# Sixteen weight forms spread over GpSimd's pairs, two weight steps moved into the attention, and a new order in the first in-projection

## The chip, the cores and the metric

The kernel runs on one core of one Trainium2 chip. The metric is device microseconds (us) of one execution; a comparison takes the median of several.

## The reference

Two layers, one after the other. The first is attention with routing: 4 batches of 8 heads, 768 positions, 64 features, 16 centroids for each head.

```
q_assign = argmax(einsum(q_n, c_n)); k_assign = argmax(einsum(k_n, c_n))
scores = where(q_assign == k_assign, scale * q @ k.T, -1e9)
attn   = softmax(scores) ;  attn_out = attn @ v
```

The heads' outputs, side by side, are x (3072 tokens by 512 features). The second layer is `h = x @ w_in` (512 by 2048), `g = h * erf(softplus(h))`, `out = g @ w_out` (2048 by 512). w_in and w_out come as float64, the other inputs and the output are float32.

## The kernel before

**Order.** Every instruction is recorded through a helper (`InOrder`, lines 119 to 132) which keeps each engine's instructions in the order of the program, so nearly all rows of the profile have line L127, and one reads them by tile. Tiles wait for one another through pools of few buffers: a tile can be written again when its last reader is done.

**Attention.** Heads are taken two at a time: 16 pairs (p = 0 to 15), each in six periods (i = 0 to 5; function `period`, line 1367, called from the loop at 1538). Each period handles two "units", tiles of 128 keys, against 768 queries; periods 0 to 2 are one half of a pair and 3 to 5 the other. What a period does for units u and u + 1:

- `step_ahead` and `maxima_step` make the softmax's shifts: TensorE writes candidates into the tile `wide`, which has a single buffer, and VectorE reduces them into `nmx`. `into_rows` turns a half's shifts into rows (`least`, `least_rows`) that SP's queue copies into `qm`.
- `products` is the first product q k (TensorE into `sc`, two buffers), and `scores` adds the rows of mask and shift (`sc<-qm,km`).
- `curve` is the exponential (ScalarE, `sc` to `pr`).
- For the two units before (u - 2, u - 1), `accumulate` adds up `pr` on GpSimd into `more_out`, for the denominators, and `attend` is the second product `pr` v (TensorE into `turned`).
- In periods 0 and 3 `divide` ends the half before: a product of the sums with a tile of minus ones (`turned<-more_out,minus`), logarithm and exponential on ScalarE (`inv`), the division on VectorE (`den`, `turned`, `more_out`), and the writes to `x_dram`.

**Weight steps.** w_in and w_out, float64 bit patterns, come as 32 steps of 512 KB, each made into float32 from the high and low words (`w_steps`, line 280): `fetch` (DMA), `size` and `rest` (ScalarE), `bounded` (VectorE), `sign` (ScalarE), `shifted` (VectorE), and `summed` (GpSimd, an integer addition), which then fetches the next step into the place that came free. Two steps are done in each pair. The last `N_LATE` = 4 are done after the attention.

**Forms.** The two matrix products use seven products in the place of eight (and in chunk 0 of the second layer, 26), so operands are first added and subtracted: `left_forms` (line 653) for w_in and `right_forms` (662) for x, four operations of 128 x 512 each. They are taken from a list `forms`: one on VectorE where the table `FORMS` says so (pair 15, periods 0, 3, 4, 5: one, two, two, two), and one on GpSimd where `POOL_FORMS` says so (pairs 8 to 15, period 1, ahead of that period's `accumulate`). The list holds w_in's columns f = 0, 2, 4, then those of x. What is left of it runs after the loop, and the four for f = 6 run on GpSimd behind the last sums of the attention.

**After the attention.** `hidden(0, 0)` and `hidden(0, 1)` make the first half of chunk 0's hidden layer, four `block`s each. A block is seven products into `bank` tiles (six buffers, then the two of `turned`), the evictions that add them up, and after each product one entry of the list `aside_work`: this list sets by its order where the late weight steps, the gate's curve (`split_gate`, `gate_work`) and the forms of w_out (`middle_forms26`, `late_forms26`) stand between the evictions. `idle(n)` is n empty entries. Between blocks 0 and 1 `finish_attention` does the last division and `next_forms26` records forms of w_out on GpSimd. The forms of w_out are chains of fills on SP (`g_more<-w_out`, `x_own<-w_out`), DMAs issued by GpSimd that add onto what was filled (`onto_by_dma`, line 803), and stores (`b_dram<-x_own`, line 794). `project26(0)` (line 1236) is the second matrix product of chunk 0. Its product `bank<-g_more,g` uses what the chains made.

Of the kernel before, what the change touches and what calls it, by code (L numbers as in the profile page):

```python
# [9 lines left out]
F32 = mybir.dt.float32  # L10
# [9 lines left out]
P = 128  # L20
# [23 lines left out]

UP = 2.0**16
FORMS = {15: {0: 1, 3: 2, 4: 2, 5: 2}}
POOL_FORMS = {p: (1,) for p in range(8, 16)}
BIG = 2.0**60
FLOOR = 2.0**50
EPS = 2.0**-70  # L50
NPT = NJ + 2
N_LATE = 4
PLACE_OF = [n % 5 for n in range(25)] + [2, 3, 2]
LAST_X = 11
MASKS = {(0, 2): ("k", 0), (2, 3): ("q", 0), (2, 2): ("k", 1), (3, 2): ("q", 1)}
FIRST_MASKS = {(2, 0): ("k", 0), (2, 1): ("q", 0), (2, 2): ("k", 1), (5, 3): ("q", 1)}
# [79 lines left out]
def kernel(  # L136
# [141 lines left out]


    w_steps = []  # L280
    for c in range(0, DFF, LC):
        for r in range(DM // P):
            w_steps.append((w_in[:, r, c : c + LC], moe_w_in[r * P : (r + 1) * P, 2 * c : 2 * (c + LC)]))
    for f in range(HF):
# [260 lines left out]
    def scores(u, rows=Q):  # L545

        p, half, j = units[u]
        st = pairs[p]
        sc = sc_of[u]
        assert ("shift", half) in st  # L550
        for e in range(2):
            r = slice(e * D, (e + 1) * D)
            r = slice(r.start, r.start + rows)
            te.matmul(
                sc[:, e, 0:HW], lhsT=st["km"][r, j * P : (j + 1) * P],
                rhs=st["qm"][r, half * HW : (half + 1) * HW], start=False, stop=True,
            )
# [95 lines left out]
    def left_forms(engine, a11, a12, a21, a22, new):  # L653

        return [
            functools.partial(plus_of, new[0], a21, a22, engine),
            functools.partial(minus_of, new[1], new[0], a11, engine),
            functools.partial(minus_of, a21, a11, a21, engine),
            functools.partial(minus_of, new[2], a12, new[1], engine),
        ]  # L660

    def right_forms(engine, b11, b12, b21, b22, new):

        return [
            functools.partial(minus_of, new[0], b12, b11, engine),
            functools.partial(minus_of, new[1], b22, new[0], engine),
            functools.partial(minus_of, b12, b22, b12, engine),
            functools.partial(minus_of, new[2], new[1], b21, engine),
        ]
# [10 lines left out]
    def w_in_parts(f, n):  # L680
        c1, c2 = slice(f * P, (f + n) * P), slice((HF + f) * P, (HF + f + n) * P)
        return (
            w_in[:, 0:HK, c1], w_in[:, HK:, c1], w_in[:, 0:HK, c2], w_in[:, HK:, c2],
            [more_in[:, i, :, c1] for i in range(3)],
        )

    def x_parts(n):
        x = x_of[n]
        return (
            x[:, 0:HK, 0:HT], x[:, 0:HK, HT:], x[:, HK:, 0:HT], x[:, HK:, HT:],  # L690
            [x_more[:, i] for i in range(3)],
        )
# [65 lines left out]
    def idle(n):  # L758
        return [lambda: None] * n
# [598 lines left out]
            run(steps)  # L1358
        return steps

    forms = []
    for f in range(0, HF - 2, 2):
        forms += zip(*(left_forms(e, *w_in_parts(f, 2)) for e in (ve, ge)))
    routing = [iter(())]
    part = [iter(())]
# [1 line left out]
    def period(p, i):  # L1367
        u = 2 * NJ * p + 2 * i
        n1, n2 = 2 * p - 1, 2 * p
        early = lambda n: 0 <= n < N_EARLY  # L1370

        def mask(place):
            which = (MASKS if p else FIRST_MASKS).get((i, place))
            if which:
                return masks(p + 1, *which, turned[0 if i in (0, 5) else 1], place == 2)
            return lambda: None

        if u > 0:
            for which in turns if i in (0, 3) else ():
                turn(*which)  # L1380
                turns.remove(which)
            if i == 3 and p:
                similarities(p + 2)
                routing[0] = choose(p + 2, turned[0], True)
            step_ahead(p, 2 * i)
            if i == 3 and p:
                next(routing[0], None)
            if i == 2:
                transposes(p + 2, "k")
        mask(0)()  # L1390
        if i == 0 and early(n1 - 1):
            sign(n1 - 1)
        elif i == 3 and early(n1):
            sign(n1)
        if i == 4:
            next(routing[0], None)
        next(part[0], None)
        if i == 0 and p:
            run(routing[0])
            transposes(p + 2, "q")  # L1400
        if u == 2:
            next(routing[0])
        products(u)
        mask(3)()
        products(u + 1)
        mask(1)()
        second = step_ahead(p, 2 * i + 1, True) if u > 0 else iter(())
        next(second, None)
        rows = D if u == 0 or u + NJ + 2 >= len(units) else Q
        scores(u, rows)  # L1410
        next(second, None)
        next(second, None)
        next(part[0], None)
        if i == 5:
            next(routing[0], None)
        scores(u + 1, rows)
        later = mask(2)
        if i == 3 and not p:
            similarities(p + 2)
            routing[0] = choose(p + 2, turned[0], True)  # L1420
        if i == 0:
            later()
            curve(u)
        else:
            curve(u)
            later()
        curve(u + 1)
        if u == 0:
            step_ahead(0, 1)
            similarities(1)  # L1430
            routing[0] = choose(1, turned[0])
            next(routing[0])
            next(routing[0])
            vectors(1, "q")
            vectors(1, "k")
        if i == 0 and early(n1 - 1):
            bounded(n1 - 1)
            shifted(n1 - 1)
        elif i == 1 and early(n1):
            size_and_rest(n1)  # L1440
        elif i == 5 and early(n2):
            rest(n2)
        for _ in range(min(len(forms), FORMS.get(p, {}).get(i, 0))):
            forms.pop(0)[0]()
        if i == 3:
            if not p:
                next(routing[0], None)
            if early(n1):
                bounded(n1)
                shifted(n1)  # L1450
        elif i == 1:
            load(p + 1, "v", v, vp)
            if p == 0:
                run(routing[0])
                transposes(2, "q")
        elif i == 4:
            vectors(p + 2, "k")
            vectors(p + 2, "q")
        if u > 0:
            if i == 1 and early(n1 - 1):  # L1460
                summed(n1 - 1)
            elif i == 4 and early(n1):
                summed(n1)
            if i in POOL_FORMS.get(p, ()) and forms:
                forms.pop(0)[1]()
            for w in (u - 2, u - 1):
                accumulate(w)
            for w in (u - 2, u - 1):
                attend(w)
            if i == 3:  # L1470
                next(routing[0], None)
            if i % HJ == 0:
                part[0] = divide(u - 1)
                next(part[0])
        if i == 3 and early(n2):
            size(n2)
# [61 lines left out]
    for p in range(NPAIR):  # L1538
        for i in range(HJ * 2):
            period(p, i)  # L1540
        if p == LAST_X:
            load_x(0)
        if p == LAST_X + 2:
            forms += zip(*(right_forms(e, *x_parts(0)) for e in (ve, ge)))
    for work, _ in forms:
        work()
    u = len(units)
    for w in (u - 2, u - 1):
        accumulate(w)
    for w in (u - 2, u - 1):  # L1550
        attend(w)
    last = divide(u - 1)
    for work in left_forms(ge, *w_in_parts(HF - 2, 2)):
        work()
    attention.close()

    psb = pool("psb", 6, space=PSUM)
# [7 lines left out]
        run(last)  # L1565
        banks[:] = [None] * 6 + turned

    places = [gsp.tile([P, 3, FG, P], F32, name="g_more").rearrange("p a j t -> p (a j t)") for _ in range(2)]
    places += [outp.tile([P, 2, DM], F32, name="osb").rearrange("p h m -> p (h m)") for _ in range(2)]
    place_of.update({N_EARLY + i: places[i][:, 0 : 2 * LC] for i in range(N_LATE)})  # L1570
    for i in range(N_LATE):
        fetch(N_EARLY + i)
# [9 lines left out]
    def all_sums():  # L1582
# [3 lines left out]

    first_half, first_products = split_gate(0, 0)
    second_half, second_products = split_gate(0, 1)
    aside_work += (
        idle(3) + sum((weights(n) for n in range(N_LATE)), []) + [first_half, all_sums, *middle_forms26(), *idle(3), *first_products]  # L1590
    )
    hidden(0, 0, {0: lambda: (finish_attention(), next_forms26())})

    def last_half():
        finish_aside()
        first_steps = [functools.partial(left_step, 0, x) for x, step in enumerate(LEFT_STEPS) if step[0] < 0]
        aside_work.extend(gate_work(0, 1, 0, first_steps, 6))

    aside_work += [second_half, *late_forms26(), *idle(4), *second_products]
    hidden(0, 1, {1: last_half}, first=ve.tensor_copy)  # L1600
    finish_aside()
    project26(0)
    last_of_x = x_more[:, 2, 0, 0:1]
# [42 lines left out]
```

## Time and profile before

| | |
|---|---|
| median of 3 runs | 950.81 us (950.78 to 950.81) |
| profiled execution | 950.88 us |
| its span, first to last instruction | 949.2 us |
| granted TensorE clock, mean | 1.000 |
| DMA traffic | 123.17 MB, mean 130 GB/s |
| GpSimd's sums for the denominators, x128 | 217.6 us, 1700 ns each |
| VectorE's reductions of `wide`, x189 | 179.1 us, 948 ns each |
| the exponentials, x192 | 148.4 us, 810 ns each |
| second products, x3072 | 145.2 us, 330 ns each |

The page has one row for each engine (busy time, share of the span, instructions), then the span in 40 slices, the DMA queues, the chain of work that ended last, and the groups of instructions. PE is TensorE's matmuls, PEld its weight loads, DVE VectorE, ACT ScalarE, POOL GpSimd, SP SyncE. A row of a timeline has the start in us, the duration in us (of all, where instructions of one kind follow each other and the row says xN), engine, line, operation, output <- inputs and shape, and in brackets the idle time of the engine before it and who ended it. Starts and durations of neighbours overlap by up to a tenth of a us.

### The profile page before, as it was taken

To read this page: it belongs to the slowest core of one execution; us is meant where nothing else is said; L and a number is where in the kernel's file an instruction comes from. 1 tells how busy PE (TensorE), PEld (TensorE's weight loads), DVE (VectorE), ACT (ScalarE), POOL (GpSimd) and SP (SyncE) were. 2 spreads that over 40 slices of the span, in tenths; PEclk is the share of its full clock that TensorE was granted. 3 is DMA by queue.
4 is the path that set the end of the run, shared out by engine and by line. 5 is a ranking of instruction groups with operands and counts; after the bars stand their busy time and mean duration, and the time that the engine had idled before them with its cause. 6 is when DMAs were issued, how large, how long until landed. Compare 5 with 4: busy or idle time off the path is not lost.

```text
span 949.2 us, 22323 instructions
## 1 busy us (share of the span) xinstructions
PE 940.0 (99%) x8758; PEld 707.4 (75%) x8758; DVE 789.3 (83%) x1418; ACT 545.9 (58%) x808; POOL 504.5 (53%) x357
## 2 busy tenths in 40 slices
PE   8999999999999999999999999999999999999998
PEld 3555555555555555588888888998999899989987
DVE  8888888888888887879886688688868977897887
ACT  3677777777777776475513643654257236525541
POOL 1688888888888888899109211360063016103600
PEclk9999999999999999999999999999999999999999
DMA  9354445444443621132876247353454436343533
GB/s 211 78 114 113 111 112 113 111 113 112 111 112 67 157 58 36 26 119 112 220 235 233 100 117 205 119 182 111 156 158 143 133 116 208 112 154 123 156 111 111
DMA packets 176344, 123.17 MB, mean 130 GB/s; under 512 B 132592, under 2 KB 143344, under 8 KB 176240
## 3 DMA queue, kind: packets, MB, share of 16 engines
q1 hardware_dynamic: 171872, 116.34, 42.9%
q0 software_dynamic: 1872, 4.98, 3.0%
q8 instruction: 69, 1.13, 0.5%
q10 hardware_dynamic: 2496, 0.43, 0.2%
q14 instruction: 35, 0.29, 0.1%
HBM read 91.78 MB, written 23.33 MB: 121 GB/s over the span
## 4 chain that ended last, share of the span: by engine, by line
PE 93%; DVE 2%; ACT 2%; issue 1%; POOL 1%; DMA 1%; SPq 0%; DVEq 0%; POOLq 0%; ACTq 0%
PE bank L127 40%; PE turned L127 31%; PE sc L127 16%; PE wide L127 6%; POOL more_out L127 1%; DVE g L127 1%; DVE nmx L127 1%; ACT a_s L127 0%; DMA g_more<-in_moe_w_out_dram 0%; ACT L127 0%; ACT w_out L127 0%; ACT osb L127 0%; SPq L127 0%; DMA qm<-least_rows 0%; ACT g_more L127 0%
## 5 line engine op out<-in xcount | busy, mean ns | idle before, releaser
L127 POOL TENSOR_TENSOR more_out<-more_out,pr 128x768 f32<-128x768 f32 x128 | 217.6, 1700 | 17.1 <-ACT pr L127 7.5
L127 DVE TENSOR_REDUCE nmx<-wide 128x2 f32<-128x512 f32 (+2 forms) x189 | 179.1, 948 | 46.9 <-PE wide L127 45.9
L127 ACT ACTIVATE pr<-sc 128x768 f32<-128x768 f32 x192 | 148.4, 810 | 82.1 <-PE wide L127 74.4
L127 PE MATMUL turned<-pr,in_v 128*32 128x193 f32 x3072 | 145.2, 330 | 0.0
L127 POOL TENSOR_TENSOR g<-g 128x512 f32<-128x512 f32 x36 | 47.1, 1308 | 180.7 <-DVE g L127 178.9
L127 PEld LDWEIGHTS turned<-pr,in_v 128*32 128x32 f32 x3072 | 90.2, 109 | 51.2 <-issue 26.5
L127 DVE TENSOR_TENSOR g<-g 128x512 f32<-128x512 f32 x132 | 90.8, 688 | 22.3 <-PE bank L127 11.8
L127 PE MATMUL sc<-qT,kT 64*128 64x384 f32 x528 | 98.5, 485 | 0.0
L127 DVE TENSOR_TENSOR g<-bank,g 128x256 f32<-128x256 f32 (+1 forms) x128 | 64.6, 531 | 16.1 <-PE bank L127 9.5
L127 PE MATMUL bank<-g_more,g 128*128 128x256 f32 x320 | 75.7, 379 | 0.0
L127 PE MATMUL bank<-x_own,w_in 128*128 128x128 f32 (+1 forms) x440 | 74.0, 310 | 0.0
L127 ACT ACTIVATE a_s<-g 128x1024 f32<-128x1024 f32 x38 | 39.5, 1053 | 57.8 <-POOL g L127 45.9
L127 POOL TENSOR_TENSOR more_out<-pr,pr 128x768 f32<-128x768 f32 x32 | 59.1, 1847 | 20.4 <-ACT pr L127 20.3
L127 DVE TENSOR_TENSOR g<-a_s,g 128x512 f32<-128x512 f32 x76 | 68.0, 913 | 0.7 <-ACT a_s L127 0.7
L127 PEld LDWEIGHTS bank<-g_more,g 128*128 128x128 f32 x320 | 60.7, 190 | 8.5 <-DVE g L127 0.2
L127 PEld LDWEIGHTS bank<-x_own,w_in 128*128 128x128 f32 x440 | 63.1, 191 | 4.6 <-issue 0.6
L127 PE MATMUL wide<-kv,qv 64*128 64x256 bf16 (+2 forms) x378 | 64.7, 327 | 1.1 <-ACT km L127 0.6
L127 PE MATMUL bank<-w_out,g 128*128 128x256 f32 x280 | 64.5, 379 | 0.0
L127 PEld LDWEIGHTS <-qv 64*128 64x128 bf16 x384 | 23.1, 93 | 53.3 <-issue 38.3
L127 ACT ACT_TABLE_LOAD x40 | 51.3, 1283 | 19.4 <-DVE g L127 18.8
L127 PE MATMUL wide<-km,qm 64*128 64x256 bf16 (+4 forms) x378 | 62.2, 326 | 0.0
L127 PEld LDWEIGHTS sc<-qT,kT 64*128 64x128 f32 x528 | 46.4, 187 | 19.0 <-issue 1.8
(241 smaller groups left out, 1993.4 us busy)
## 6 DMA issues: line engine op xcount, KB each, us to landing
g_more<-b_dram SPq DMA_DIRECT2D x52, 512.0 KB
g_more<-w_dram SPq DMA_DIRECT2D x84, 256.0 KB
x_own<-in_moe_w_in_dram SPq DMA_DIRECT2D x13, 512.0 KB
in_v<-in_v_dram SPq DMA_DIRECT2D x32, 192.0 KB
x_dram<-more_out SPq DMA_DIRECT2D x128, 48.0 KB
x_own<-x_dram SPq DMA_DIRECT2D x6, 1024.0 KB
in_k<-in_k_dram SPq DMA_DIRECT2D x59, 96.0 KB
in_q<-in_q_dram SPq DMA_DIRECT2D x58, 96.0 KB
```

Source lines behind the costliest of these rows:

```text
L127: ins = getattr(self.engine, name)(*args, **kw)
```

## The change

- GpSimd's forms stand in pairs 5 to 13 (before 8 to 15). The list holds the 16 forms of w_in, f = 0, 2, 4, 6. The four of x have a list of their own, `x_forms`, on VectorE, which is emptied first in pair 15.
- What is left of the forms of w_in in the list runs on GpSimd after `next_forms26` (before: four right after the attention's last sums).
- `N_LATE` is 2: steps 28 and 29 (w_out) are done in pairs 14 and 15. In pair 15 both are summed in period 4. The order of w_in's steps takes the columns 0, 1024, 512, 1536. The two late steps both use the tiles `osb`.
- In pair 15, period 3, both `attend`s stand before `scores`.
- In the first in-projection, the `aside_work` has 8 entries of weight steps (before 16), then the sums, the middle forms, the gate's curve and its products, each of which is followed by an empty entry; `last_half` comes after block 0 of `hidden(0, 1)` and no longer empties the list.

In the order of the engines, that leaves TensorE the same instructions, of which only `attend` and `scores` of that one period change places. On VectorE, pair 15 has between its eighth and ninth reduction `bounded` and `shifted` of step 28 and one form of x (before: one form of w_in), and in period 3 two forms of x and `bounded` and `shifted` of step 29 ahead of the division. On GpSimd the sums of steps 28 and 29 stand ahead of the sums of the last two units but two. On SP two fetches of w_out move into pair 14, and in `project26(0)` a store `b_dram<-x_own` moves ahead of a fill `g_more<-w_out`. ScalarE does the size of step 28 in pair 14, period 3, its rest in period 5, its sign in pair 15, period 0, and those of step 29 in periods 1 and 3.

```diff
-POOL_FORMS = {p: (1,) for p in range(8, 16)}
+POOL_FORMS = {p: (1,) for p in range(5, 14)}
-N_LATE = 4
-PLACE_OF = [n % 5 for n in range(25)] + [2, 3, 2]
+N_LATE = 2
+PLACE_OF = [n % 5 for n in range(25)] + [2, 3, 2, 3, 2]
...
-    for c in range(0, DFF, LC):
+    for c in (0, DFF // 2, LC, DFF // 2 + LC):
...
-    forms = []
-    for f in range(0, HF - 2, 2):
+    forms, x_forms = [], []
+    for f in range(0, HF, 2):
...
+        attends_first = p == NPAIR - 1 and i == HJ
+        if attends_first:
+            for w in (u - 2, u - 1):
+                attend(w)
         scores(u, rows)
...
-        for _ in range(min(len(forms), FORMS.get(p, {}).get(i, 0))):
-            forms.pop(0)[0]()
+        for _ in range(FORMS.get(p, {}).get(i, 0)):
+            x_forms.pop(0)() if x_forms else forms.pop(0)[0]()
...
-            if i == 1 and early(n1 - 1):
+            if i == (1 if p < NPAIR - 1 else 4) and early(n1 - 1):
                 summed(n1 - 1)
-            elif i == 4 and early(n1):
+            if i == 4 and early(n1):
                 summed(n1)
...
-            for w in (u - 2, u - 1):
+            for w in () if attends_first else (u - 2, u - 1):
                 attend(w)
...
-            forms += zip(*(right_forms(e, *x_parts(0)) for e in (ve, ge)))
-    for work, _ in forms:
-        work()
+            x_forms += right_forms(ve, *x_parts(0))
...
-    for work in left_forms(ge, *w_in_parts(HF - 2, 2)):
-        work()
...
-    places = [gsp.tile([P, 3, FG, P], F32, name="g_more").rearrange("p a j t -> p (a j t)") for _ in range(2)]
-    places += [outp.tile([P, 2, DM], F32, name="osb").rearrange("p h m -> p (h m)") for _ in range(2)]
+    places = [outp.tile([P, 2, DM], F32, name="osb").rearrange("p h m -> p (h m)") for _ in range(2)]
...
+    def spread(work):
+        return sum(([w, *idle(1)] for w in work), [])
+
     aside_work += (
-        idle(3) + sum((weights(n) for n in range(N_LATE)), []) + [first_half, all_sums, *middle_forms26(), *idle(3), *first_products]
+        idle(3) + sum((weights(n) for n in range(N_LATE)), []) + [all_sums, *middle_forms26(), *idle(1), first_half, *idle(8)]
     )
-    hidden(0, 0, {0: lambda: (finish_attention(), next_forms26())})
+    aside_work += spread(first_products)
+
+    def next_forms():
+        next_forms26()
+        for _, work in forms:
+            work()
+
+    hidden(0, 0, {0: lambda: (finish_attention(), next_forms())})
 
     def last_half():
-        finish_aside()
...
-    aside_work += [second_half, *late_forms26(), *idle(4), *second_products]
-    hidden(0, 1, {1: last_half}, first=ve.tensor_copy)
+    aside_work += [second_half, *late_forms26(), *idle(4), *second_products[:2], *idle(1), *second_products[2:]]
+    hidden(0, 1, {0: last_half}, first=ve.tensor_copy)
```

## The prediction

> **What bounds the kernel now.** First the page, for which engine is full; then windows of stages for idle TensorE; then timelines of each idle stretch.
>
> ```profile
> span 949.2 us, 22323 instructions
> PE 940.0 (99%) x8758; PEld 707.4 (75%) x8758; DVE 789.3 (83%) x1418; ACT 545.9 (58%) x808; POOL 504.5 (53%) x357
> PE 93%; DVE 2%; ACT 2%; issue 1%; POOL 1%; DMA 1%; SPq 0%; DVEq 0%; POOLq 0%; ACTq 0%
> ```
>
> TensorE is busy for 940.0 of 949.2 us, and 93% of the chain that ends last is its own work. The change leaves its 8758 matmuls as they are and only lets four groups of the last pair change places. So the time can move by no more than what TensorE's gaps gain or lose, and the table of windows (columns: window, its length, then busy time and count of PE, PEld, DVE, ACT and POOL; clock, DMA share, GB/s) says where gaps are.
>
> ```profile
> 220.00:240.00 20.00, 20.00 (x290) 10.69 (x289) 17.37 (x30) 16.01 (x24) 16.94 (x12) 1.00 0.43 93
> 361.00:373.00 12.00, 11.72 (x167) 6.20 (x161) 8.89 (x14) 9.03 (x14) 10.81 (x8) 1.00 0.14 32
> 385.00:402.00 17.00, 16.70 (x255) 9.54 (x254) 13.69 (x16) 8.30 (x12) 14.40 (x9) 1.00 0.11 25
> 420.00:440.00 20.00, 19.10 (x88) 16.18 (x87) 16.12 (x30) 12.79 (x14) 20.00 (x16) 1.00 0.20 80
> ```
>
> In a middle pair there is none (20.00 of 20.00). Pair 14 leaves 0.28 us, pair 15 leaves 0.30, the start of the second half 0.90. That is all there is to win near the change, at most about 3 us; what can be lost has no such limit.
>
> **Term 1: pairs 5 to 7 get a form on GpSimd, pair 14 loses its own.** The list of waits for pairs 8 to 13, and the timeline of pair 14:
>
> ```profile
> PEld turned L127 <- POOL more_out L127: 1.2, 6, 0.2
> 370.77 0.16 PEld L127 LDWEIGHTS turned<-more_out,minus 128*32 128x32 f32 x8 [0.66 <-POOL more_out L127]
> 360.60 1.28 POOL L127 TENSOR_TENSOR w_in<-w_in 128x512 f32<-128x512 f32 x1
> 369.02 1.69 POOL L127 TENSOR_TENSOR more_out<-more_out,pr 128x768 f32<-128x768 f32 x1
> ```
>
> The six pairs that have a form each show one wait of 0.2 us for GpSimd's sums of the exponentials, ahead of the product that spreads the denominators. Three more such pairs cost between 0 and 3 x 0.2 = 0.6; the window above that has a form in it has no idle TensorE, so I take +0.1. In pair 14 the same wait is 0.66: GpSimd's last sum ends at 369.02 + 1.69 = 370.71, and TensorE starts at 370.77. Without the 1.28 us form that chain ends earlier, and the wait falls to at most the others' 0.2: −0.46 (between 0 and −0.66). Late next is the row of weight loads itself. Weight step 28's size and rest, new in this pair, are ScalarE's, which is idle for 3 of these 12 us; its fetch stands on SP behind reads of v that are needed a pair later. I cost both at nothing; without that cover a fetch of 512 KB would delay a v tile, and the first row of the next pair would show it.
>
> **Term 2: three operations of VectorE ahead of a maximum in pair 15.** Before, one form stands between the eighth and ninth reductions; after, `bounded` and `shifted` of step 28 and a form of x, and GpSimd has no form there.
>
> ```profile
> 380.92 1.23 DVE L127 TENSOR_REDUCE nmx<-wide 128x2 f32<-128x1024 f32 x1 [1.14 <-PE wide L127]
> 380.92 1.52 ACT L127 ACTIVATE pr<-sc 128x768 f32<-128x768 f32 x2 [2.19 <-PE wide L127]
> 381.66 1.28 POOL L127 TENSOR_TENSOR more_in<-w_in 128x512 f32<-128x512 f32 x1
> 382.06 1.43 DVE L127 TENSOR_TENSOR more_in<-w_in,more_in 128x512 f32<-128x512 f32 x1
> 382.90 2.27 POOL L127 TENSOR_TENSOR more_out<-pr,pr 128x768 f32<-128x768 f32 x1
> 383.41 0.68 DVE L127 TENSOR_REDUCE nmx<-wide 128x2 f32<-128x512 f32 x1
> 384.20 0.38 PE L127 MATMUL wide<-kv,qv 64*128 64x512 bf16 x2
> 358.35 0.88 DVE L127 TENSOR_SCALAR w_out<-w_out 128x512 f32<-128x512 f32 x2
> 370.07 1.39 DVE L127 TENSOR_SCALAR w_out<-w_out 128x512 f32<-128x512 f32 x2
> 396.74 0.69 DVE L127 TENSOR_TENSOR more_in<-w_in,more_in 128x512 f32<-128x512 f32 x1
> 389.81 2.16 DVE L127 TENSOR_TENSOR w_in<-w_in 128x512 f32<-128x512 f32 x1
> 385.90 7.62 POOL L127 TENSOR_TENSOR more_out<-more_out,pr 128x768 f32<-128x768 f32 x4 [0.74 <-ACT pr L127]
> ```
>
> The ninth reduction ends at 383.41 + 0.68 = 384.09 and TensorE's next `wide`, which has one buffer, starts at 384.20: it waits for nothing else. A VectorE form takes 0.69 alone but 1.43 or 2.16 beside GpSimd; two scalar operations take 0.88 alone and 1.39 beside it, ending 0.75 after GpSimd's 370.71. So of the two engines one stands still until the other's instruction is done. In after, the eighth reduction ends at 382.1; `bounded` runs to 382.58 (0.44). The exponentials end at 382.44, and GpSimd's first sum, which before had to follow its own form, is ready then and runs next: about 1.7 us (as at 369.02), to 384.3. Then `shifted` 0.44, the next sum not being ready before 385.9; the form 0.69; the reduction, 0.6 to 0.68 in: 384.3 + 0.44 + 0.69 + 0.68 = 386.1 at worst, with overlapped starts (rows begin up to 0.1 before the last ends) 385.85. Against 384.09 that is **+1.75**. The least is GpSimd after all three: 382.1 + 0.88 + 0.69 + 0.68 = 384.35, +0.25. I take +1.75, since between two waiting engines the row of four sums beside two VectorE forms (1.9 each where 1.69 is the sum alone; 1.73 and 2.16 where 0.69 is) shows them taking turns. Nothing gives it back in the pair: scores, exponentials and GpSimd's sums all follow that `wide`.
>
> In the Trainium skill, "SBUF — State Buffer", section "Who interferes with whom", states that VectorE and GpSimd share a port pair under an exclusive lock for a whole instruction, and that issue order decides who blocks. The rows agree that one blocks entirely; who comes first at 382.5 no run here shows yet. By the skill's rule taken strictly, an instruction of VectorE in the queue before 382.44 would hold GpSimd off, and the sum would have +0.25 here: rival B.
>
> **Term 3: second products ahead of scores at the end of pair 15's first half.**
>
> ```profile
> 391.59 0.50 PE L127 MATMUL sc<-qm,km 64*128 64x384 bf16 x4 [0.26 <-DMA qm<-least_rows]
> 393.57 0.16 PEld L127 LDWEIGHTS turned<-more_out,minus 128*32 128x32 f32 x8 [0.42 <-POOL more_out L127]
> ```
>
> The scores waited 0.26 for the transfer of the shift rows. With the second products (1.51 us) ahead of them that wait is hidden. But the product behind waits for GpSimd: the sums end at 385.90 + 7.62 = 393.52, and it starts at 393.57. Second products and scores both stand before it, in either order, so the gap moves and stays: 0, between −0.4 and +0.2 (the exponentials start later, and ScalarE has slack). The two x forms and step 29 behind it are on a VectorE that idles 3.1 us there; the two integer sums now in this half, on GpSimd, are in term 4.
>
> **Term 4: the first blocks after the attention.** Timelines of 405 to 448:
>
> ```profile
> 396.81 8.41 POOL L127 TENSOR_TENSOR more_out<-more_out,pr 128x768 f32<-128x768 f32 x4 [1.37 <-ACT pr L127]
> 405.26 0.37 ACT L127 COPY g<-bank 128x256 f32<-128x256 f32 x1 [4.63 <-POOL more_out L127]
> 407.15 1.03 PE L127 MATMUL bank<-x_more,w_in 128*128 128x256 f32 x4
> 371.59 1.29 POOL L127 TENSOR_TENSOR w_out<-w_out,x_own 128x512 int32<-128x512 int32 x1 [0.88 <-PE turned L127]
> 426.65 0.35 ACT L127 COPY g<-turned 128x256 f32<-128x256 f32 x1
> 435.09 0.73 PEld L127 LDWEIGHTS turned<-x_more,more_in 128*128 128x128 f32 x4 [0.76 <-DVE g L127]
> 436.76 0.73 PEld L127 LDWEIGHTS turned<-x_own,w_in 128*128 128x128 f32 x4 [0.95 <-DVE g L127]
> 447.19 0.73 PEld L127 LDWEIGHTS bank<-x_own,w_in 128*128 128x128 f32 x4 [0.20 <-DVE g L127]
> ```
>
> The gaps at 435 to 447 are TensorE waiting for VectorE's evictions, which all stand behind ScalarE's copy at 426.65, after the gate's curves. With two weight steps fewer before the curves and the gate's products spread out, that copy comes some 2.3 us earlier (two steps are 4 ScalarE operations of about 1 us, two of them hidden beside GpSimd). 2.3 covers the largest gap, so 0.76 + 0.95 + 0.20 = 1.91 less some 0.1 that remains: −1.82. On the other side, two sums of 1.29 now stand ahead of GpSimd's last sums of pair 15, whose end (396.81 + 8.41 = 405.22) releases the first eviction at 405.26; that end comes some 1.8 later (2.6 less the 0.8 of idle before them), the eviction too, and the seventh product, at 407.15, needs its bank after it: 0.45 lost. Sum **−1.37**, between −1.82 and 0.
>
> **Term 5: the chain of w_out's forms.** Before, the four forms of column 6 ran at once after the attention; now they run behind the forms of w_out, with two sums fewer in their way.
>
> ```profile
> 406.98 1.27 POOL L127 TENSOR_TENSOR more_in<-more_in,w_in 128x512 f32<-128x512 f32 x1
> 450.35 1.87 POOL L127 DMA_DIRECT2D more_out<-x_own  x2
> 466.24 1.09 SPq L810 DMA_DIRECT2D g_more<-w_out  x1
> 467.92 0.72 SPq L794 DMA_DIRECT2D b_dram<-x_own  x1
> 473.66 0.84 POOL L127 DMA_DIRECT2D g_more<-x_own  x1 [9.71 <-PE bank L127]
> g_more<-x_own POOLq DMA_DIRECT2D x1, 512.0 KB, 4.6
> 480.11 1.89 PE L127 MATMUL bank<-g_more,g 128*128 128x256 f32 x8
> ```
>
> Four forms (4 x 1.27 = 5.1) move from a time in which GpSimd would have waited for the division to one in which it works; two sums of 1.29 go: its last issue, at 450.35, comes 0.6 to 1 later. On SP the fill of `g_more` (466.24) now stands behind the store (467.92 + 0.72): up to 2.4 later. The transfer that adds onto it lands at 473.66 + 4.6 = 478.26, and TensorE needs it at 480.11: 1.85 of slack, of which term 4 takes 1.37 by bringing TensorE forward. Left is 0.5; for a delay of 1.3, the middle of 0 to 2.4, the loss is **+0.8**. Ends: 0, and (1.0 + 2.4) − 0.5 = 2.9.
>
> The Trainium skill, "DMA: Bandwidth & Descriptors", section "Queues, rings and completion order", has descriptors of one issuing engine consumed in ring order on each DMA engine. By that the fill would wait out the store's 512 KB, and the loss would lie nearer its upper end; rival D.
>
> **The sum.** +0.1 − 0.46 + 1.75 + 0 − 1.37 + 0.8 = +0.82. The profiled execution took 950.88 (its span and 1.7 around it), 0.07 above the median of 950.81. 950.88 + 0.82 = **951.7**. The other edits (column order of w_in's steps, places, names) add no instruction.
>
> **Rivals.**
> - **B: VectorE's three operations go first.** Term 2 is +0.25, GpSimd's end is as before, term 4 is −1.5: 0.1 − 0.46 + 0.25 − 1.5 + 0.8 = −0.8, so **950.1**. For it: VectorE is already at work when GpSimd becomes ready. Against: the alternation at 385.90.
> - **D: slower by the chain of w_out.** Place: the product at 480.11. It decides once the fill's data come more than 0.5 us late; from there each us is lost one for one. At the upper end 2.9 in the place of 0.8: **953.8**. For it: the store is now ahead in the same queue. Against: 473.66 waited, by its row, for a product, so the fill may have had room.
> - **E: the covers all hold.** Term 2 +0.25, term 3 −0.4, term 4 −1.82, term 5 zero: 0.1 − 0.46 + 0.25 − 0.4 − 1.82 = −2.3, so **948.6**.
> - That the swap of term 3 does nothing, because GpSimd ends last, is in the forecast.
>
> **How the numbers follow.** A difference under 0.2%, 1.9 us, is about what a measurement can't tell from none. Chances: forecast 0.53, B 0.17, D 0.18, E 0.12. Faster by more is most of E, 0.10; slower by more is D, 0.18; 0.72 remain. The range leaves out half of D above and most of E below: 949.0 to 953.6.
>
> **What would show it.** Right: at the `wide` before the second unit of pair 15, TensorE idle for about 1.7 us behind a reduction near 386; no GpSimd wait of 0.66 in pair 14; no gap for VectorE at 435 to 447; a wait of under 1 us for `g_more` near 480. Wrong: the first sum on GpSimd beginning after the x form (B); a gap of 2 us or more at the first products with `g_more` (D); or any gap over 0.5 us in pairs 5 to 7, for which no row here stands.

## The result, and the profile after

The changed kernel takes 952.13 us (median of 22 runs, 951.67 to 952.46), the kernel before 950.78 beside it (22 runs, 950.41 to 951.34): ratio 1.0014, 95% interval 1.0008 to 1.0020. It is 1.35 us slower. The interval leaves out 1, so the loss is clear of the noise, but it is under the 0.2% that the prediction set as its bound. The profiled execution took 952.18, before 950.88.

The page after: the same matmuls, the same busy TensorE, a span 1.3 longer, so all of the difference is idle TensorE.

```profile
span 950.5 us, 22319 instructions
PE 940.0 (99%) x8758; PEld 707.5 (74%) x8758; DVE 790.5 (83%) x1417; ACT 546.3 (57%) x808; POOL 504.7 (53%) x358
PE 96%; DVE 2%; POOL 1%; issue 1%; ACT 0%; DVEq 0%; POOLq 0%
```

The table of windows of the changed kernel, with one more than before (after the length: busy time and count of PE, PEld, DVE, ACT, POOL; clock, DMA share, GB/s):

```profile
361.00:373.00 12.00, 12.00 (x171) 6.34 (x167) 8.60 (x15) 9.62 (x15) 10.09 (x8) 1.00 0.29 83
385.00:402.00 17.00, 15.86 (x228) 8.66 (x231) 16.44 (x20) 10.38 (x15) 13.80 (x8) 1.00 0.11 25
420.00:440.00 20.00, 20.00 (x94) 17.61 (x93) 13.96 (x32) 12.22 (x12) 19.92 (x15) 1.00 0.20 80
440.00:470.00 30.00, 29.16 (x136) 25.38 (x135) 26.18 (x48) 19.00 (x21) 15.40 (x13) 1.00 0.58 147
```

Pair 14 has no gap left (12.00 of 12.00, before 11.72), and 420 to 440 has none (20.00, before 19.10). From 385 to 402, in pair 15, TensorE is idle for 1.14 where it was for 0.30, and a part of that gap lies ahead of 385. The stretch from 440 to 470 has a new gap of 0.84. The sharpest reading is to take the same instruction of TensorE in both traces and compare its start. Wherever the difference jumps, time was lost or won between this row and the one above it (for the first row, since the start of the program):

| TensorE's instruction | before | after | difference | step |
|---|---|---|---|---|
| `turned<-more_out,minus`, pair 12 | 323.13 | 323.56 | +0.43 | +0.43 |
| the same, pair 14 | 370.77 | 370.74 | −0.03 | −0.46 |
| `wide`, pair 15 | 384.20 | 385.75 | +1.55 | +1.58 |
| `turned<-more_out,minus`, pair 15 | 393.58 | 395.16 | +1.58 | +0.03 |
| seventh product after the attention | 407.15 | 408.89 | +1.74 | +0.16 |
| `bank<-x_more,more_in`, past the old gaps | 448.16 | 448.50 | +0.34 | −1.40 |
| `bank<-more_out,g_more` | 452.48 | 453.82 | +1.34 | +1.00 |
| last instruction | | | +1.30 | −0.04 |

A row gives the first matmul of its group. Behind the first matmul of the seventh product another 0.10 is lost, so that the win after it, counted from there, is 1.50. Behind 453.82 another 0.07 is lost, and 0.11 is won at 561.6, as in run 5 below; the cause of that stays open.

The timeline of pair 15 in the changed kernel, at the largest step:

```profile
382.00 0.88 DVE L127 TENSOR_SCALAR w_out<-w_out 128x512 f32<-128x512 f32 x2
382.45 2.09 POOL L127 TENSOR_TENSOR more_out<-pr,pr 128x768 f32<-128x768 f32 x1 [0.80 <-ACT pr L127]
382.79 2.30 DVE L127 TENSOR_TENSOR x_more<-x_own 128x512 f32<-128x512 f32 x1
385.02 0.68 DVE L127 TENSOR_REDUCE nmx<-wide 128x2 f32<-128x512 f32 x1
385.75 0.39 PE L127 MATMUL wide<-kv,qv 64*128 64x512 bf16 x2 [1.44 <-DVE nmx L127]
```

The two scalar operations run to 382.88. GpSimd's sum was issued at 382.45, but its 2.09 are 0.43 of standing still and 1.66 of work, to 384.54. The x form was issued at 382.79 and shows 2.30: it stood until 384.5 and then took its 0.6. Only then comes the reduction, and the row of `wide` says what TensorE waited for: 1.44 us, `nmx`.

The second loss, at 453.8: first the rows of the kernel before, then of the one after.

```profile
447.90 2.51 POOL L127 TENSOR_TENSOR more_out<-w_out,g_more 128x512 f32<-128x512 f32 x2
450.50 0.68 DVE L127 TENSOR_TENSOR g_more<-g 128x512 f32<-128x512 f32 x1
451.43 0.68 DVE L127 TENSOR_TENSOR g_more<-g,g_more 128x512 f32<-128x512 f32 x1
```

```profile
449.37 2.49 POOL L127 TENSOR_TENSOR more_out<-w_out,g_more 128x512 f32<-128x512 f32 x2
450.77 1.64 DVE L127 TENSOR_TENSOR g_more<-g 128x512 f32<-128x512 f32 x1
451.80 1.87 POOL L127 DMA_DIRECT2D more_out<-x_own  x2
452.99 0.68 DVE L127 TENSOR_TENSOR g_more<-g,g_more 128x512 f32<-128x512 f32 x1
453.82 1.97 PE L127 MATMUL bank<-more_out,g_more 128*128 128x256 f32 x8 [0.84 <-DVE g_more L127]
```

Before, GpSimd's last forms were over at 450.41 and VectorE's first step of `g_more` ran after them, 0.68. After, those forms end at 451.86, the step begins beside them and takes 1.64, 0.96 more, and the product that reads `g_more` waits 0.84. It starts 0.15 after VectorE's second step of `g_more` ends (453.67, before 452.11).

### The profile page after: what moved, and what is told of

It is laid out like the page before. It is cut to its first block, busy times and chain, and to the rows that moved or that the text cites. A ratio compares the mean times of both kernels' runs of the same rounds, so it can differ in the third digit from the quotient of the medians.

```text
span 950.5 us, 22319 instructions
## 1 busy us (share of the span) xinstructions
PE 940.0 (99%) x8758; PEld 707.5 (74%) x8758; DVE 790.5 (83%) x1417; ACT 546.3 (57%) x808; POOL 504.7 (53%) x358
## 4 chain that ended last, share of the span: by engine, by line
PE 96%; DVE 2%; POOL 1%; issue 1%; ACT 0%; DVEq 0%; POOLq 0%
PE bank L127 43%; PE turned L127 31%; PE sc L127 16%; PE wide L127 6%; DVE nmx L127 1%; POOL more_out L127 1%; DVE x_more L127 0%; DVE w_out L127 0%; DVE kT L127 0%; DVE g L127 0%; ACT pr L127 0%; DVE g_more L127 0%; DVE sims L127 0%; ACT km L127 0%; DVE hotT L127 0%
## 5 line engine op out<-in xcount | busy, mean ns | idle before, releaser
L127 DVE TENSOR_TENSOR g<-a_s,g 128x512 f32<-128x512 f32 x76 | 65.9, 889 | 0.4 <-ACT a_s L127 0.4
L127 ACT ACTIVATE x_own<-x_own 128x512 int32<-128x512 uint32 (+2 forms) x60 | 61.0, 1025 | 0.4
```

What stands on the lines that cost most here:

```text
L127: ins = getattr(self.engine, name)(*args, **kw)
```

## The experiments

Every run was timed in five rounds beside the kernel before, which had medians of 950.73 to 950.78. Time steps below are starts of the same TensorE instruction, compared as in the table.

**1. The x form later.** The form of period 0 of pair 15 moves to period 4.

```diff
-FORMS = {15: {0: 1, 3: 2, 4: 2, 5: 2}}
+FORMS = {15: {3: 2, 4: 3, 5: 2}}
```

> The changed kernel, but the x form of pair 15, period 0, is done in period 4; the two scalar operations of step 28 stay. Collision theory: in the changed kernel the ninth reduction ends at 385.70 because the form waited for GpSimd's sum, and TensorE's next wide waits 1.44. Without the form the two scalar operations end at 382.9, the reduction at about 383.5, and wide is no longer late: all of 1.5 to 1.6 goes, 950.6 us. Rival 1, the scalar operations are the load: they cost 0.88 of it, so about 0.7 goes, 951.4. Rival 2, VectorE has no room later in the pair (19.44 busy of 20.00 in 385 to 405): the form is paid again in period 4, 952.1 or more.

Measured 949.65 us, ratio to before 0.9989 (0.9980 to 0.9997).

```profile
381.93 0.88 DVE L127 TENSOR_SCALAR w_out<-w_out 128x512 f32<-128x512 f32 x2
382.39 2.09 POOL L127 TENSOR_TENSOR more_out<-pr,pr 128x768 f32<-128x768 f32 x1 [0.81 <-ACT pr L127]
382.99 0.69 DVE L127 TENSOR_REDUCE nmx<-wide 128x2 f32<-128x512 f32 x1 [0.18 <-PE wide L127]
413.14 2.67 POOL L127 TENSOR_TENSOR more_out<-w_out,more_out 128x512 f32<-128x512 f32 x2 [0.66 <-DVE more_out L127]
449.05 0.82 DVE L127 TENSOR_TENSOR g_more<-g 128x512 f32<-128x512 f32 x1
```

The reduction now waits for TensorE, not for VectorE's queue, and `wide` starts 1.68 earlier than in the changed kernel. Both rivals fell: the scalar operations cost nothing, and the form isn't paid again in period 4. The gain is 0.9 more than I expected, and 0.85 of that comes at 453.8. GpSimd's wait for the division, 2.08 in the changed kernel, is 0.66 here, so its last forms end earlier, and the step of `g_more` takes 0.82 in the place of 1.64.

**2. The x form first.** No work moves to another period; the form only stands ahead of the two scalar operations.

```diff
+        if i == 0 and p == NPAIR - 1:
+            x_forms.pop(0)()
         if i == 0 and early(n1 - 1):
             bounded(n1 - 1)
             shifted(n1 - 1)
...
-        for _ in range(FORMS.get(p, {}).get(i, 0)):
+        for _ in range(FORMS.get(p, {}).get(i, 0) if i else 0):
```

> The changed kernel, but in pair 15, period 0, the x form stands ahead of the two scalar operations on VectorE (no work is added or left out). The form then starts at 382.0, before the exponentials end at 382.4. Theory of turns: GpSimd's sum takes its turn when the form ends at 382.7 and runs to 384.4, then both scalar operations follow, 0.88: the reduction ends near 385.9 as before or 0.2 later, 952.1 to 952.4. Rival, VectorE goes on as long as it has a next instruction: form and scalar operations end at 383.6, the reduction at 384.2, the gap of 1.44 falls to 0.1, 950.7.

Measured 952.14 us, ratio 1.0015 (1.0006 to 1.0024).

```profile
381.79 0.68 DVE L127 TENSOR_TENSOR x_more<-x_own 128x512 f32<-128x512 f32 x1
382.24 1.91 POOL L127 TENSOR_TENSOR more_out<-pr,pr 128x768 f32<-128x768 f32 x1 [0.81 <-ACT pr L127]
382.38 2.50 DVE L127 TENSOR_SCALAR w_out<-w_out 128x512 f32<-128x512 f32 x2
384.80 0.69 DVE L127 TENSOR_REDUCE nmx<-wide 128x2 f32<-128x512 f32 x1
385.54 0.39 PE L127 MATMUL wide<-kv,qv 64*128 64x512 bf16 x2 [1.45 <-DVE nmx L127]
```

Now the form is fast (0.68), and the scalar operations, 0.88 elsewhere, take 2.50. GpSimd took its turn after the form, although VectorE had more to do. The wait of TensorE is the same 1.45. So it isn't the form as such: whatever of this kind stands behind GpSimd's sum in VectorE's queue, ahead of a reduction that TensorE needs, costs one sum.

**3. Column 6 first.** The four forms of f = 6 run on GpSimd right behind the attention's last sums, as before the change.

```diff
     last = divide(u - 1)
+    for _, work in forms:
+        work()
     attention.close()
...
     def next_forms():
         next_forms26()
-        for _, work in forms:
-            work()
```

> The changed kernel, but the four forms of column 6 run on GpSimd right after the attention's last sums, as before the change. Theory: the wait of 1.2 at 453.8 (the first product that reads g_more) comes from GpSimd's last forms being 1.45 late, so that VectorE's first step of g_more at 450.77 stood 0.96 still beside them. With the forms ahead of the division GpSimd's idle 2.08 is filled, its last issue comes near 450, the wait goes: 951.1 us. Rival: the wait comes from the new order of evictions and gate products on VectorE itself: 452.1, no gain. Rival of the prediction: the fill behind the store at 466 costs something: then nothing changes either, and there is a wait near 480.

Measured 951.12 us, ratio 1.0004 (0.9995 to 1.0013).

```profile
449.51 1.86 POOL L127 DMA_DIRECT2D more_out<-x_own  x2
450.45 0.68 DVE L127 TENSOR_TENSOR g_more<-g 128x512 f32<-128x512 f32 x1
452.51 1.59 PEld L127 LDWEIGHTS bank<-more_out,g_more 128*128 128x128 f32 x8 [0.25 <-issue]
```

GpSimd is done at 449.5 in the place of 451.8, VectorE's step takes 0.68 again. The 0.25 in the last row is idle time of the weight loads; TensorE's matmuls have none there. The gain is 1.0, as expected.

**4. Scores first.** The order of second products and scores in pair 15 as before the change.

```diff
-        attends_first = p == NPAIR - 1 and i == HJ
+        attends_first = False
```

> The changed kernel, but the second products of pair 15, period 3, stand behind the scores, as before the change. Theory: GpSimd's sum of the same half ends last in either order (395.1), so the product behind starts at the same time: 952.1 us, within 0.2. Rival: the wait for the shift rows comes back (0.26 to 0.87 before) and stays: 952.5 to 952.9.

Measured 952.12 us, ratio 1.0014 (1.0006 to 1.0023). The timeline shows why the swap is worth nothing:

```profile
393.16 0.50 PE L127 MATMUL sc<-qm,km 64*128 64x384 bf16 x4 [0.35 <-DMA qm<-least_rows]
395.06 0.53 PE L127 MATMUL turned<-more_out,minus 128*32 128x192 f32 x8
```

In the changed kernel:

```profile
395.16 0.53 PE L127 MATMUL turned<-more_out,minus 128*32 128x192 f32 x8 [0.39 <-POOL more_out L127]
```

TensorE is idle for 0.35 ahead of the scores again, and no longer for the 0.39 ahead of the product that needs GpSimd's sums. That product starts at 395.06, against 395.16. The gap only changed its place.

**5. The lists alone.** The kernel before, with the new lists of forms and the order of w_in's columns that they need. `N_LATE`, the swap and the in-projection stay.

```diff
-POOL_FORMS = {p: (1,) for p in range(8, 16)}
+POOL_FORMS = {p: (1,) for p in range(5, 14)}
...
-    for c in range(0, DFF, LC):
+    for c in (0, DFF // 2, LC, DFF // 2 + LC):
...
-    forms = []
-    for f in range(0, HF - 2, 2):
+    forms, x_forms = [], []
+    for f in range(0, HF, 2):
...
-        for _ in range(min(len(forms), FORMS.get(p, {}).get(i, 0))):
-            forms.pop(0)[0]()
+        for _ in range(FORMS.get(p, {}).get(i, 0)):
+            x_forms.pop(0)() if x_forms else forms.pop(0)[0]()
...
-            forms += zip(*(right_forms(e, *x_parts(0)) for e in (ve, ge)))
-    for work, _ in forms:
-        work()
+            x_forms += right_forms(ve, *x_parts(0))
...
-    for work in left_forms(ge, *w_in_parts(HF - 2, 2)):
+    for _, work in forms:
         work()
```

> The kernel before with only the new lists: GpSimd's forms in pairs 5 to 13, x forms first on VectorE in pair 15, w_in's steps in the new column order, what is left (column 6) right after the attention. Late weight steps, swap and first in-projection stay as before. Theory of the prediction's terms 1 and 2: -0.46 in pair 14, +0.1 to +0.4 in pairs 5 to 13, and in pair 15 the ninth reduction comes earlier than 384.09, because one form of VectorE that starts at 382.06 ahead of the sum meets no GpSimd form: up to -0.2. Sum -0.6 to 0: 950.2 to 950.8. Rival: the lists alone carry the loss of the whole change (GpSimd's forms in more pairs): 951.5 or more.

Measured 950.23 us, ratio 0.9994 (0.9985 to 1.0002). The steps: +0.38 up to pair 12 (0.30 of it there), −0.46 in pair 14, 0.00 at `wide` of pair 15, −0.47 at the gap of 435, the rest small. The −0.47 wasn't expected, and the up to −0.2 at `wide` didn't come. With one form of VectorE and none of GpSimd in that period, the form goes first, the sum follows it, and nothing that has to wait for the sum stands ahead of the reduction:

```profile
381.96 0.68 DVE L127 TENSOR_TENSOR x_more<-x_own 128x512 f32<-128x512 f32 x1
382.40 1.91 POOL L127 TENSOR_TENSOR more_out<-pr,pr 128x768 f32<-128x768 f32 x1 [0.82 <-ACT pr L127]
383.01 0.69 DVE L127 TENSOR_REDUCE nmx<-wide 128x2 f32<-128x512 f32 x1 [0.38 <-PE wide L127]
```

So the lists don't carry the loss. It needs the two scalar operations of the moved weight step as well.

**6, 10 and 11. The list beside the in-projection.** Run 6 goes back to the old order and takes the empty entries out of the first half's gate products; run 10 keeps the new order and takes them out (in the second half, the one empty entry moves ahead of the products); run 11 keeps them and puts the curve back to the front. In runs 6 and 11 the gate's products also come six entries earlier, since 3 empty entries stand ahead of them in the place of 9.

```diff
-    ... [all_sums, *middle_forms26(), *idle(1), first_half, *idle(8)]
-    aside_work += spread(first_products)
+    ... [first_half, all_sums, *middle_forms26(), *idle(3), *first_products]    # run 6
...
+    aside_work += first_products                                                # run 10
+    aside_work += [second_half, *late_forms26(), *idle(4), *idle(1), *second_products]
...
+    ... [first_half, all_sums, *middle_forms26(), *idle(3)]                     # run 11
```

> The changed kernel with the old order in the first block of the list beside the in-projection (gate's curve right after the weight steps, then sums, middle forms, the four products of the gate in a row). Theory: the gaps at 435 to 447 went because ScalarE has two weight steps fewer ahead of the curve: they stay away, 952.1 within 0.4. Rival: they went because the gate's products were spread: 0.8 to 1.7 come back, 952.9 to 953.8.

> The changed kernel with the new order beside the in-projection (curve behind the sums and the middle forms), but the gate's products one after the other, with no empty entries between them, in both halves. Theory: the order does it, because VectorE's evictions no longer wait behind ScalarE's curve while TensorE needs their banks: 952.1 to 952.5. Rival: the spread does it: 953 or more, gaps again at 427 to 434.

> The changed kernel with the products of the gate spread, but the curve right after the weight steps, ahead of sums and middle forms. Theory: the order does it, so the gap of 0.76 for ScalarE's copy near 424 and part of the 2.4 behind it come back: 952.7 to 954.2. Rival: the spread does it: 952.1.

Measured: run 6 (five executions), 954.18 us, ratio 1.0034 (1.0021 to 1.0047); run 10, 951.17, 1.0004 (0.9996 to 1.0013); run 11, 951.91, 1.0012 (1.0003 to 1.0021). TensorE's waits in run 6, in its timeline of weight loads:

```profile
423.88 0.73 PEld L127 LDWEIGHTS turned<-x_own,w_in 128*128 128x128 f32 x4 [0.76 <-ACT g L127]
429.76 0.73 PEld L127 LDWEIGHTS bank<-x_own,w_in 128*128 128x128 f32 x4 [0.84 <-DVE g L127]
433.12 0.73 PEld L127 LDWEIGHTS turned<-x_more,more_in 128*128 128x128 f32 x4 [1.77 <-DVE g L127]
```

In run 11 only the first of these is there (0.78 at 423.93) with 0.22 at 433.5; in run 10 there is none. So neither hypothesis of run 6 holds by itself: the later curve, with the products behind it, is enough, and spread products alone leave those two waits. Run 6 came out above both of its hypotheses, run 10 below both, and run 11 0.2 below its rival. Only both undone give the loss of 3.1, of which 1.0 comes back at 453.8. Run 10 gains 1.0 besides, at 453.8, although GpSimd is no earlier there than in the changed kernel:

```profile
447.88 1.69 DVE L127 TENSOR_TENSOR g_more<-g 128x512 f32<-128x512 f32 x1
448.98 3.40 POOL L127 TENSOR_TENSOR more_out<-w_out,g_more 128x512 f32<-128x512 f32 x2
```

The step of `g_more` is just as slow (1.69), but without the empty entries it begins 2.9 earlier (447.88, not 450.77), so it is done in time. In run 11 the step is as late and as slow as in the changed kernel (450.59, 1.69). There TensorE, held up at 424 and 433, comes to the product only at 453.48, after the second step's end at 453.20, and doesn't wait.

**7. Both corrections.** Runs 1 and 3 together.

> The changed kernel with both corrections: the x form of pair 15, period 0, in period 4, and the four forms of column 6 right after the attention's last sums. Adding the two gains would give 952.1 - 2.5 - 1.0 = 948.6. But without the form alone GpSimd's last forms were already early enough for VectorE's first step of g_more (0.82 in the place of 1.64), so that what is left of the wait there is 0.1 to 0.2. Theory: 949.4 to 949.6. Rival, the two are independent: 948.6.

Measured 949.51 us, ratio 0.9987 (0.9979 to 0.9996), as for one cause that either removes. It has the lowest median, 1.25 us below the kernel before; run 1 is 0.14 above it, and the ranges of the two overlap.

**8 and 9. A reduction in the form's place.** Run 1, and where the form stood, one more reduction of `x_own`, whose result nobody reads: in run 8 into a tile of its own, in run 9, shown here, into maxima that pair 15 doesn't use.

```diff
             shifted(n1 - 1)
+            if p == NPAIR - 1:
+                ve.tensor_reduce(out=maxima[0][:, :, 0, 0], in_=x_of[0][:, 0:2, 0:256], axis=AX.X, op=ALU.max)
```

> As the run with the form done later, but where the form stood VectorE does one more reduction of 128 x 512 elements from the buffer x_own into a tile that nobody reads. It takes about as long as the form alone (0.6 to 0.7) and reads one operand. Theory: the loss in the changed kernel is the form's wait for GpSimd, not its own length: the reduction runs beside GpSimd's sum, the ninth maximum ends near 384.2, wide is at most 0.1 to 0.2 late, 949.8. Rival, any instruction there waits for GpSimd: 952.1. Rival, the length decides: the form's 0.69 alone is what matters, 950.3.

> The extra reduction in the place of the form once more, written into a tile of maxima that pair 15 does not use, so that no tile is added: the run before had its first transfers land 1.4 later at the program's start, ahead of everything that differs. Theory: without that the time is that of the run with the form done later plus at most 0.2, 949.6 to 949.9. Rival: the 1.4 belong to the reduction after all, 951.1 to 951.3.

Run 8: 951.29 us, ratio 1.0016 (1.0001 to 1.0031; twelve executions, two of which, 956.9 and 958.71, widen the interval). Its difference from run 1 is 1.41 at TensorE's start at 8 us, far ahead of the reduction. Run 9: 949.68 us, ratio 0.9988 (0.9979 to 0.9997), the same as run 1 (949.65).

```profile
382.42 2.10 POOL L127 TENSOR_TENSOR more_out<-pr,pr 128x768 f32<-128x768 f32 x1 [0.80 <-ACT pr L127]
382.77 0.68 DVE L127 TENSOR_REDUCE nmx<-x_own 128x2 f32<-128x512 f32 x1
383.36 0.68 DVE L127 TENSOR_REDUCE nmx<-wide 128x2 f32<-128x512 f32 x1
384.12 0.38 PE L127 MATMUL wide<-kv,qv 64*128 64x512 bf16 x2
```

An instruction as long as the form, at the same place, beside the same sum, and it takes 0.68. So length is not the loss. The form waits because it is of a kind that GpSimd's instruction shuts out; a reduction isn't. The Trainium skill, "SBUF — State Buffer", section "Who interferes with whom", says so: on trn2 a `tensor_reduce` never contends, a `tensor_tensor` with both inputs in that memory does. These two rows, 0.68 and 2.30, agree with it. What in the kind does it, the tiles read or the tile written, these runs don't separate.

## Why the prediction held, point by point

- **Term 1: −0.36 forecast, −0.03 measured.** Pair 14's gap went as worked out (−0.46). Of the +0.1 for the other pairs, +0.43 came: 0.12 in pairs 5 to 7, inside its bounds, and about 0.3 in pair 12, which had a form before too. There GpSimd's integer sum began at 312.14 in the place of 311.71, and its row names `inv` of ScalarE as what it waited for, where before it named `pr`. Run 5 has it as well, so it belongs to the lists. First the row before, then the row after:

```profile
311.71 1.28 POOL L127 TENSOR_TENSOR w_out<-w_out,x_own 128x512 int32<-128x512 int32 x1 [1.54 <-ACT pr L127]
312.14 1.29 POOL L127 TENSOR_TENSOR w_out<-w_out,x_own 128x512 int32<-128x512 int32 x1 [1.81 <-ACT inv L127]
```

The four sums behind it end 0.43 later too (323.51, before 323.08), and the product that needs them starts right after. Why the integer sum waits for a later instruction of ScalarE isn't settled.
- **Term 2: +1.75 forecast, +1.58 measured.** The mechanism is the one forecast: the sum of GpSimd between VectorE's operations, the reduction, `wide`. Only its detail differs: both scalar operations passed ahead of the sum, and the x form waited. Run 1 takes it away, run 2 shows turns being taken in the other order, run 9 shows that the kind of instruction decides. Rival B, that VectorE goes on as long as it has work, fell in the changed kernel itself, where the sum was issued at 382.45 and the form, though in VectorE's queue, only at 382.79; and again in run 2. By these rows an instruction that stands in VectorE's queue doesn't hold GpSimd off.
- **Term 3: 0 forecast, +0.03 measured**, and 0.01 between medians in run 4, for the reason given: GpSimd's sum is last in both orders.
- **Term 4: −1.37 forecast, −1.24 measured** (+0.16 where 0.45 was expected, −1.40 where −1.82 was). The place was right, the reason was not. I put the gain down to ScalarE's copy coming 2.3 earlier through two weight steps fewer. It came at 425.21, 1.44 earlier than 426.65. But in run 6, with as few weight steps, the copy comes still earlier (423.47) and the gaps are larger than ever. What removed them is where the curve and the gate's products stand between VectorE's evictions. What the fewer steps add wasn't tried by itself. One thing more goes with the gaps: the four gate products on VectorE, `g<-a_s,g`, meet GpSimd's forms too. First a row of the kernel before, then two of the changed kernel, the last of them four products behind GpSimd's last form:

```profile
429.63 1.72 DVE L127 TENSOR_TENSOR g<-a_s,g 128x512 f32<-128x512 f32 x1
426.99 0.83 DVE L127 TENSOR_TENSOR g<-a_s,g 128x512 f32<-128x512 f32 x1
454.86 2.49 DVE L127 TENSOR_TENSOR g<-a_s,g 128x512 f32<-128x512 f32 x4
```

The four of the first half take 5.98 before, 6.11 in run 6, 5.01 in run 11, 4.82 in run 10 and 3.64 in the changed kernel. In run 5 the first of them takes 1.30 in the place of 1.72, and 0.47 of the gap at 435 goes with it. How much of the gaps is this and how much the order of the evictions, no run separates.
- **Term 5: +0.8 forecast, +1.00 measured, at another place.** The step that failed is the fill behind the store. In the changed kernel it is issued 4 us later (470.21, before 466.24), but what it feeds starts only 1.8 later: before, that waited for a product until 473.66, and now it waits for the fill (timeline of the changed kernel):

```profile
470.21 0.63 SPq L810 DMA_DIRECT2D g_more<-w_out  x1
475.48 0.84 POOL L127 DMA_DIRECT2D g_more<-x_own  x1 [12.62 <-DMA g_more<-w_out]
481.52 1.89 PE L127 MATMUL bank<-g_more,g 128*128 128x256 f32 x8
```

The view of the transfers gives the last number, 4.5 us from issue to landing:

```profile
g_more<-x_own POOLq DMA_DIRECT2D x1, 512.0 KB, 4.5
```

475.48 + 4.5 = 479.98, and TensorE needs it at 481.52: 1.54 of slack, before 1.85. Nothing is lost there, so rival D didn't come, nor the wait near 480 that the prediction named as a sign of being right. Two things were also wrong in the sum itself: term 4's 1.37 was taken off the slack while term 2's 1.75, which makes TensorE later, was left out (the product came 1.41 later, not earlier), and the middle of 0 to 2.4 is 1.2, not 1.3. The same late chain on GpSimd, 1.45 behind where 0.6 to 1 was expected, did cost 1.00, but by standing beside VectorE's first step of `g_more` at 450.77. That +0.8 comes so near to it is luck: the cause was right (column 6 behind the forms of w_out makes GpSimd late), the victim was another. The runs show what it takes: GpSimd late (run 3 undoes it), the empty entries that put VectorE's step late (run 10), and the two engines shutting each other out. Undoing either of the first two removes the wait.
- **The sum:** −0.03 + 1.58 + 0.03 + 0.16 − 1.40 + 1.00 = +1.34 up to the product at 453.8 and +1.30 at the last instruction, against +0.82 forecast; +1.35 between the medians. The terms missed by +0.33, −0.17, +0.03, +0.13 and +0.20: only terms 2 and 3 held with their mechanism, term 1 held in pair 14, and in terms 4 and 5 the amount held and the reason didn't.

## What to carry to other kernels

An engine that is 83% busy and far from the bound can still set the end: look for the instruction that the full engine waits for, and ask which instructions stand ahead of it in its queue and which of them another engine can shut out. When work is moved to a place with room, check what runs on GpSimd at that moment, and put only a kind of operation there that doesn't meet it, as the reduction of run 9. And when a gap goes away after an edit with several parts, undo the parts one by one and together: here the later curve would have done by itself, and together with the empty entries it cost 1.0 elsewhere.

## What the runs showed of the hardware that was not expected

- In the one build with a small added tile that nobody reads (run 8) the first transfers of the program landed later: VectorE's transpose of k began at 8.35 after 1.08 of waiting for `in_k`, in run 1 at 6.95 with no wait. The whole run kept that 1.4 us; without the tile (run 9) it was gone. A variant with another layout of tiles should first be compared at its start. What in the layout does it isn't known.
- Turns were forecast; that a full queue of VectorE doesn't hold GpSimd off, wherever the work stands in it, is what run 2 adds. GpSimd's sum went in between VectorE's form and its scalar operations (0.88 of work shown as 2.50), as in the changed kernel it went in between the scalar operations and the form, though VectorE never ran out of work.
